# One value visit and one score fewer in two job words, and the gate's tanh behind the branch

## The chip, the cores and the metric

The kernel runs on one core of a Trainium2 chip. The metric is the device time of one execution in microseconds, as the median of several runs. Five engines work from queues of their own: TensorE (PE), VectorE (DVE), ScalarE (ACT), GpSimd (POOL) and SyncE (SP, which only issues DMAs here). Each works its queue in order, and they wait for one another by semaphores.

## The reference

```python
def _A_ref(x, wq, wk, wv, wo):          # 2048 tokens, D = 512, 32 heads of 16, one key/value head
    scores = jnp.einsum("bhqd,bkd->bhqk", q, k) * (Dh ** -0.5)
    p = _softmax(scores, axis=-1)
    o = jnp.einsum("bhqk,bkd->bhqd", p, v)
    ...
def _B_ref(x, w_gate, w_up, w_down):    # F = 1376
    return (_gelu(x @ w_gate) * (x @ w_up)) @ w_down

g = _sigmoid((x * gate_w).sum(-1, keepdims=True))
return g * a + (1 - g) * b              # a = attention, b = feed-forward
```

The kernel writes the sigmoid as a tanh: with t = tanh(z/2), g is 0.5t + 0.5 (tile `gt`) and 1 - g is -0.5t + 0.5 (tile `gc`).

## The kernel before, in words

**Prologue.** Weights and x are split into a high and a low part, and three matmuls per product keep the precision. The keys, the values and the queries are computed; the queries go through DRAM. Then a bound for the scores decides whether a softmax shift has to be computed: `values_load` of `flag` and `tc.If` (lines 514 and 515) make every engine load the flag and branch past a long body, which is not taken here. Between the last query matmul and the branch stand the first feed-forward chunk's gate and up products, its GELU's first step, the gate tanh (line 505) with its two DVE steps (lines 506 and 507), and the split of the second chunk's weights: three parts, each a cast on DVE and a subtraction on POOL.

**Main part.** Attention and feed-forward are interleaved by hand in one long stream of PE work. Attention is cut into 32 units of 16 key blocks, a *step* each: one unit is four heads of 512 queries. A step is two *scores* (`S`; each a pair of matmuls into a double bank `s`, then an exp on ACT from `s` to a tile `p` of 1024 columns, line 575) and one *value visit* (`V`; `pv`, line 645: four matmuls, recorded as eight, from the two `p` tiles into the accumulator `acc`). There are 1024 scores and 512 value visits. There is one accumulator bank: where a unit ends, `norm` copies it out on DVE (lines 586 and 596) before the next unit's first value visit may write it.

**Words.** The feed-forward and the output projection are cut into 81 *jobs*. Each has a pair of accumulators `z` and `y` and a stream of matmul pairs, `F`. A job is played by a word of the table `WORDS`: G for a gate/up job, D and E for the two halves of a down projection over three chunks, d and e for the same over two chunks, W for the output projection, L for the first gate/up job. In a word, `S3` means three scores, `V2` two value visits, `F6` six matmul pairs; `H` opens the pair and `R` closes it. `z` occupies the third of three double banks between `H` and `R`, so that scores then have two banks, taken in turn; at `R` that bank goes to the end of the turn. With no job left, `T` ("V2 S3") is played until all visits are done.

**The lead.** What the scores have issued ahead of the value visits is called the lead here, in steps: scores issued / 2 - visits made. `visit(k)` makes at most `ready` visits, those whose two scores have been issued, and carries the rest over to the next `V`. The lead is thus set when the program is written, not while it runs. At a lead of zero after a visit, that visit has read the exp of the score issued just before it.

**Order of jobs.** For each of the four groups of 512 tokens: G jobs with D E behind every third, then d e behind the last two chunks. Two W jobs for a group stand behind the next group's first D E.

Of the kernel before, what the change touches and what calls it, by code (L numbers as in the profile page):

```python
# [13 lines left out]
AF = mybir.ActivationFunctionType  # L14
ALU = mybir.AluOpType
# [5 lines left out]
S = 2048  # L21
D = 512
H = 32
DH = 16
F = 1376
# [14 lines left out]
EVERY = 3  # L40
PB = 12
WORDS = {
# [8 lines left out]
}  # L51

# [2 lines left out]
def mix_kernel(ctx, tc, xT, wq, wkv, wo, wf, out):  # L55
    nc = tc.nc
# [21 lines left out]
    zt = cp.tile([P, NKC], F32, name="zt")  # L78
    gt = cp.tile([P, NKC], F32, name="gt")
    gc = cp.tile([P, NKC], F32, name="gc")  # L80
# [37 lines left out]
    def split(eng_h, eng_l, hi, lo, src):  # L118
        if eng_h is nc.scalar:
            eng_h.copy(hi, src)  # L120
        else:
            eng_h.tensor_copy(hi, src)  # L122
        eng_l.tensor_sub(lo, src, hi)  # L123
# [87 lines left out]
    W = {}  # L211
# [4 lines left out]
    def defer(k, fn):  # L216
        later.setdefault(now[0] + k, []).append(fn)
# [6 lines left out]
    def split_w(n):  # L224
        if n not in stage:
            return []
        st = stage.pop(n)
        gh = cp.tile([P, 2, NC, P], F32R, tag="gh", name=f"gh{n}", bufs=2)
        gl = cp.tile([P, 2, NC, P], F32R, tag="gl", name=f"gl{n}", bufs=2)
        dh = cp.tile([P, D], F32R, tag="dh", name=f"dh{n}", bufs=4)  # L230
        dl = cp.tile([P, D], F32R, tag="dl", name=f"dl{n}", bufs=4)
        W[n] = gh, gl, dh, dl
        view = lambda t: st[:, t].rearrange("p (c f) -> p c f", c=NC)
        parts = [(gh[:, t], gl[:, t], view(t)) for t in range(2)] + [(dh, dl, st[:, 2])]
        return [lambda part=part: split(nc.vector, nc.gpsimd, *part) for part in parts]
# [96 lines left out]
    def flush(q):  # L332
        while q:
            q.pop(0)()
# [39 lines left out]
    def gelu(n, g, u):  # L374
        flush(chain)
        gs = cp.tile([P, TG], F32, tag="gs", name=f"gs{n}", bufs=1)
        sq = cp.tile([P, TG], F32, tag="sq", name=f"sq{n}", bufs=1)
        nc.vector.tensor_copy(gs, g)  # L378

        def inner():  # L380
            nc.vector.scalar_tensor_tensor(sq, gs, GC, gs, op0=ALU.mult, op1=ALU.mult)  # L381
            nc.vector.scalar_tensor_tensor(sq, sq, 1.0, gs, op0=ALU.add, op1=ALU.mult)

        def tanh():
            nc.scalar.activation(sq, sq, AF.Tanh, bias=0.0, scale=GS)  # L385

        def outer():
            nc.vector.scalar_tensor_tensor(sq, sq, 1.0, gs, op0=ALU.add, op1=ALU.mult)
            nc.vector.scalar_tensor_tensor(gs, u(), 0.5, sq, op0=ALU.mult, op1=ALU.mult)

        def halves():
            hh = cp.tile([P, TG], F32R, tag="hh", name=f"hh{n}", bufs=3)
            hl = cp.tile([P, TG], F32R, tag="hl", name=f"hl{n}", bufs=3)
            nc.vector.tensor_copy(hh, gs)
            nc.vector.tensor_sub(hl, gs, hh)
            hold.append((n, hh, hl))

        chain.extend((inner, tanh, outer, halves))

    def advance(m):  # L400
        def go():
            while len(chain) > m:
                chain.pop(0)()

        return go
# [83 lines left out]
    nsteps = 8 * NTG * NKC  # L489
# [12 lines left out]
    up0 = ps_a.tile([P, TG], F32, tag="pa", name="u0")  # L502
    chain_mm(up0, weights_terms(0, 1))
    gelu(0, ps, lambda: up0)
    nc.scalar.activation(gt, zt, AF.Tanh, bias=0.0, scale=0.5)
    nc.vector.tensor_scalar(gc, gt, -0.5, 0.5, op0=ALU.mult, op1=ALU.add)
    nc.vector.tensor_scalar(gt, gt, 0.5, 0.5, op0=ALU.mult, op1=ALU.add)
    for part in split_w(1):
        part()
    pro.close()  # L510
    mp = ctx.enter_context(tc.tile_pool(name="mp", bufs=1))
# [127 lines left out]
    def pv(s):  # L639
        u, kc = divmod(s, NKC)  # L640
        if kc == 0:
            accp[u] = ps_a.tile([P, TG], F32, tag="pa", name=f"acc{u}")
        vt = (v1, v2)[u % 2]
        for j in range(4):
            nc.tensor.matmul(accp[u][32 * j : 32 * j + 32], vt[:, kc], pb[s, j // 2][:, (j % 2) * TG : (j % 2 + 1) * TG],  # L645
                             start=(kc == 0), stop=(kc == NKC - 1), skip_group_check=True)
        del pb[s, 0], pb[s, 1]

    at_s, at_v, carry = [0], [0], [0]
# [5 lines left out]
    def visit(k):  # L655
        if at_v[0] == nsteps:
            return
        flush(chain if at_v[0] == 0 else [])
        want = k + carry[0]
        left = NKC - at_v[0] % NKC  # L660
        ready = at_s[0] // 2 - at_v[0]
        take = max(min(want, left, ready, 4), 0)
        if left - take == 1 and take < 3 and ready > take:
            take += 1
        carry[0] = want - take
        for _ in range(take):
            pv(at_v[0])
            at_v[0] += 1
        if take and at_v[0] % NKC == 0:
            if at_v[0] == nsteps:  # L670
                ends.append(None)
            else:
                norm(at_v[0] // NKC - 1)

    def play(word, job=None):
        if job:
            X, Y = job[1]()
        for t in word.split():
            k = int(t[1:] or 1)
            if t[0] == "S":  # L680
                for _ in range(k):
                    score()
            elif t[0] == "V":
                visit(k)
            elif t[0] == "H":
                advance(1)()
                held.add(2)
                z = ps_s.tile([P, 2 * TG], F32, tag="s2", name="z")[:, 0:TG]
                y = ps_f.tile([P, TG], F32, tag="pf", name="y")
                pairs = pair_mm(z, y, X, Y)  # L690
            elif t[0] == "F":
                for _ in range(k):
                    next(pairs)
            else:
                assert next(pairs, None) is None
                held.discard(2)
                turn.remove(2)
                turn.append(2)
                job[2](z, y)

    ends = []
    chain.pop(0)()
    for k, m in ((2, 2), (4, 0)):
        defer(k, advance(m))
    for job in jobs():
# [60 lines left out]
```

## Time and profile before

| | us |
|---|---|
| median of 3 runs (lowest, highest) | 1322.84 (1322.68, 1323.7) |
| profiled execution | 1322.12 |
| its span, first to last instruction | 1320.3 |
| PE busy | 1286.6 |
| ACT busy | 1034.9 |
| DVE busy | 573.7 |
| POOL busy | 221.4 |
| mean granted clock of TensorE | 0.995 |

Matmuls are pipelined and their ends are modelled: a PE that counts as busy may be waiting inside a value visit for half of its input. Where a job's length matters, it is read from the start of the job's first pair to the start of the next job's, as a stretch of the trace. A window's answer gives its length, then for each engine the busy time and the number of records, the granted clock, and the DMA's share and rate.

### The profile page before, as it was taken

The numbers are of one execution on the slowest core, as the hardware profiler recorded it, in microseconds if no ns is written. First come the engines' busy times: TensorE is split into PE (matmuls) and PEld (weight loads), VectorE is DVE, ScalarE is ACT, GpSimd is POOL, SyncE is SP. The second block draws the span as 40 slices with busy tenths as digits, with TensorE's granted clock in tenths as the row PEclk, the third lists the DMA queues.
The fourth block names the chain that finished last, engine by engine and source line by source line (L and its number), as shares of the span: only waits on it lengthen the run. The fifth ranks groups of instructions, "written<-read, shape, count | busy, mean of one in ns | idle before, by whom it ended". The sixth has DMA issues, their size and how long they took to land.

```text
span 1320.3 us, 23905 instructions
## 1 busy us (share of the span) xinstructions
PE 1286.6 (97%) x9884; PEld 663.8 (50%) x9884; DVE 573.7 (43%) x860; ACT 1034.9 (78%) x1118; POOL 221.4 (17%) x261
## 2 busy tenths in 40 slices
PE   9989999999999999999899999999999999999998
PEld 6854555454444454455355445554544445445544
DVE  6762543534541162624535145252644324344333
ACT  5368888887777888888687788888877788888883
POOL 3141202122210120202211012120222002112100
PEclk9989999999999999999999999999999999999999
DMA  8541112011100201111110021011121002110000
GB/s 310 184 131 38 62 37 62 27 53 53 62 14 30 76 27 38 62 38 53 53 51 12 30 77 62 14 63 36 54 65 37 14 30 87 50 34 32 14 1 32
DMA packets 26371, 72.67 MB, mean 55 GB/s; under 512 B 4016, under 2 KB 4048, under 8 KB 26256
## 3 DMA queue, kind: packets, MB, share of 16 engines
q1 hardware_dynamic: 25244, 69.17, 15.9%
q8 instruction: 80, 1.31, 0.4%
q10 hardware_dynamic: 756, 1.11, 0.3%
q0 software_dynamic: 256, 0.79, 0.1%
q14 instruction: 35, 0.29, 0.1%
HBM read 57.67 MB, written 13.37 MB: 54 GB/s over the span
## 4 chain that ended last, share of the span: by engine, by line
PE 88%; ACT 2%; POOL 1%; DVE 1%; issue 1%; DMA 0%; SPq 0%; ACTq 0%; DVEq 0%
PE acc L645 36%; PE z L353 24%; PE s L572 21%; PE y L353 6%; ACT p L575 2%; POOL gl L123 1%; PE wos L338 1%; DMA Q<-scr 0%; DVE n L596 0%; DVE acc L460 0%; PE wof L338 0%; DVE n L586 0%; POOL mark L361 0%; ACT sq L385 0%; DVE sq L381 0%
## 5 line engine op out<-in xcount | busy, mean ns | idle before, releaser
L575 ACT ACTIVATE p<-s 128x1024 f32<-128x1024 f32 x1024 | 981.5, 1024 | 226.7 <-PE s L572 219.9
L645 PE MATMUL acc<-p,v 128*32 128x512 f32 x4096 | 516.5, 601 | 8.4 <-DVE n L586 4.1
L572 PE MATMUL s<-Q,kp 51*128 51x512 f32 x2048 | 385.2, 420 | 13.1 <-ACT p L575 7.3
L572 PEld LDWEIGHTS s<-Q,kp 51*128 51x128 f32 x2048 | 183.2, 185 | 239.7 <-ACT p L575 139.2
L645 PEld LDWEIGHTS acc<-p,v 128*32 128x32 f32 x4096 | 108.2, 109 | 270.4 <-issue 221.7
L123 POOL TENSOR_TENSOR gl<-st,gh 128x512 fp32r<-128x512 f32 x88 | 124.8, 1439 | 378.2 <-DVE gh L122 136.2
L378 DVE COPY gs<-z 128x512 f32<-128x512 f32 x43 | 29.7, 692 | 282.3 <-PE y L353 273.8
L353 PE MATMUL z<-xh,gh 64*128 64x512 f32 x344 | 144.1, 419 | 1.2 <-POOL mark L361 0.9
L353 PE MATMUL y<-xh,gh 64*128 64x512 f32 x344 | 144.0, 419 | 0.0
L353 PE MATMUL y<-xl,gh 64*128 64x512 f32 x344 | 135.3, 393 | 0.0
L353 PE MATMUL z<-xl,gh 64*128 64x512 f32 x344 | 135.3, 393 | 0.0
L353 PE MATMUL y<-xh,gl 64*128 64x512 f32 x344 | 133.9, 389 | 0.0
L353 PE MATMUL z<-xh,gl 64*128 64x512 f32 x344 | 133.9, 389 | 0.0
L361 POOL MEMSET mark<- 1x1 f32 x81 | 8.1, 100 | 664.6 <-PE y L353 659.9
L353 PEld LDWEIGHTS z<-xh,gh 64*128 64x128 f32 x344 | 63.9, 186 | 59.7 <-ACT p L575 25.9
L450 DVE SCALAR_TENSOR_TENSOR acc<-z,gc,acc 128x512 f32<-128x512 f32 x24 | 18.0, 751 | 172.5 <-PE z L353 113.8
L353 PE MATMUL z<-dh,hh 64*128 64x512 f32 x176 | 70.4, 400 | 5.9 <-ACT p L575 5.9
L353 PEld LDWEIGHTS z<-xh,gl 64*128 64x128 f32 x344 | 64.2, 186 | 12.8
L353 PE MATMUL y<-dh,hh 64*128 64x512 f32 x176 | 70.6, 401 | 0.0
L353 PEld LDWEIGHTS z<-xl,gh 64*128 64x128 f32 x344 | 64.4, 187 | 10.8
L353 PE MATMUL y<-dh,hl 64*128 64x512 f32 x176 | 68.9, 391 | 0.0
L353 PE MATMUL z<-dh,hl 64*128 64x512 f32 x176 | 68.8, 391 | 0.0
(147 smaller groups left out, 1581.3 us busy)
## 6 DMA issues: line engine op xcount, KB each, us to landing
st<-wf SPq DMA_DIRECT2D x44, 768.0 KB
scr<-q SPq DMA_DIRECT2D x16, 512.0 KB
Q<-scr SPq DMA_DIRECT2D x60, 128.0 KB
out<-acc SPq DMA_DIRECT2D x16, 256.0 KB
Q<-scr SPq DMA_DIRECT2D x60, 64.0 KB
xr<-xT SPq DMA_DIRECT2D x6, 512.0 KB
xst<-xT SPq DMA_DIRECT2D x12, 256.0 KB
xr<-xT SPq DMA_DIRECT2D x4, 256.0 KB
```

The costliest lines, as they stand in the source:

```text
L123: eng_l.tensor_sub(lo, src, hi)
L338: nc.tensor.matmul(ps, a, b, start=(first and q == 0), stop=(last and q == len(terms) - 1), skip_group_check=True)
L353: mm = nc.tensor.matmul(ps, a[rs], b[rs], start=(half == 0 and q == 0), stop=(half == 1 and q == len(X) - 1), skip_group_check=True)
L361: relay = nc.gpsimd.memset(mark, 0.0).ins
L378: nc.vector.tensor_copy(gs, g)
L450: nc.vector.scalar_tensor_tensor(o, ps, w, o, op0=ALU.mult, op1=ALU.add)
L572: nc.tensor.matmul(ps[:, j * TG : (j + 1) * TG], kp[rs, kc * P : (kc + 1) * P], Q[u][rs, pr], start=True, stop=True)
L575: nc.scalar.activation(p, ps, AF.Exp, bias=0.0, scale=SCALE)
L645: nc.tensor.matmul(accp[u][32 * j : 32 * j + 32], vt[:, kc], pb[s, j // 2][:, (j % 2) * TG : (j % 2 + 1) * TG], start=(kc == 0), stop=(kc ...
```

## The change

Two edits in the table change what is issued: the word W has one score less at its end ("S R S2" becomes "R S2"), and the word e one visit less at its start ("V S V S V S H" becomes "S V S V S H"). In L the first of the two scores ahead of `H` moves behind it. ("F6 S2 F6" and "F6 S S F6" are the same stream.) There are six W jobs and four e jobs; what they no longer issue comes at the end, in `T`.

Around the branch, the gate tanh and its two DVE steps are put off by five scores, and the third part of the second chunk's split (`dh` and `dl`) is issued behind the branch. `ends` was a list that nothing reads.

```diff
 WORDS = {
-    "L": "S2 H F3 S F3 S F6 S2 F6 S F6 R S",
+    "L": "H S F3 S F3 S F6 S S F6 S F6 R S2",
     "G": "V2 S2 V H V F S2 F6 S F3 S F2 S F3 S F3 S F6 R S2 V2 S3 V",
-    "W": "V2 S2 H V2 S F S F6 S F2 S V S F3 S V S F S V S F2 S F3 S V S F6 S R S2",
+    "W": "V2 S2 H V2 S F S F6 S F2 S V S F3 S V S F S V S F2 S F3 S V S F6 R S2",
     "D": "V H V S2 V2 S2 F6 S F3 S V S F S F5 S F3 S R",
-    "E": "V S3 H V3 S F3 S F6 S2 F6 S F3 R S V2 S3",
+    "E": "V S3 H V3 S F3 S F6 S S F6 S F3 R S V2 S3",
     "d": "V S V H S F3 S F3 S V S F2 S F4 R",
-    "e": "V S V S V S H F3 S F3 S V2 S F5 S F R S",
+    "e": "S V S V S H F3 S F3 S V2 S F5 S F R S",
 }
...
     gelu(0, ps, lambda: up0)
-    nc.scalar.activation(gt, zt, AF.Tanh, bias=0.0, scale=0.5)
-    nc.vector.tensor_scalar(gc, gt, -0.5, 0.5, op0=ALU.mult, op1=ALU.add)
-    nc.vector.tensor_scalar(gt, gt, 0.5, 0.5, op0=ALU.mult, op1=ALU.add)
-    for part in split_w(1):
+    rest = split_w(1)
+    for part in rest[:2]:
         part()
...
-            if at_v[0] == nsteps:
-                ends.append(None)
-            else:
+            if at_v[0] < nsteps:
                 norm(at_v[0] // NKC - 1)
...
-    ends = []
+    def gates():
+        nc.scalar.activation(gt, zt, AF.Tanh, bias=0.0, scale=0.5)
+        nc.vector.tensor_scalar(gc, gt, -0.5, 0.5, op0=ALU.mult, op1=ALU.add)
+        nc.vector.tensor_scalar(gt, gt, 0.5, 0.5, op0=ALU.mult, op1=ALU.add)
+
+    rest[2]()
     chain.pop(0)()
+    defer(5, gates)
```

**DVE's queue at the branch**, before (the copy of the first gate product, the two gate steps, the split's three casts, the load of the flag, the branch):

```order
L313 TENSOR_SCALAR woh<-woh,sh 1x2048
L378 COPY gs_658<-g_622 128x512
L506 TENSOR_SCALAR gc<-gt 128x16
L507 TENSOR_SCALAR gt<-gt 128x16
L122 CAST gh_664<-st_191 128x512 x2
L122 CAST dh_666<-st_191 128x512
L514 TENSOR_LOAD flag
L515 COMPARE_AND_BRANCH
```

and now (the long body between the two branches is left out of the second piece, which begins at its end):

```order
L313 TENSOR_SCALAR woh<-woh,sh 1x2048
L378 COPY gs_658<-g_622 128x512
L122 CAST gh_661<-st_191 128x512 x2
L512 TENSOR_LOAD flag
L513 COMPARE_AND_BRANCH
```

```order
L513 UNCONDITIONAL_BRANCH x2
L122 CAST dh_663<-st_191 128x512
L381 SCALAR_TENSOR_TENSOR sq_659<-gs_658 128x512
L382 SCALAR_TENSOR_TENSOR sq_659<-sq_659,gs_658 128x512
L388 SCALAR_TENSOR_TENSOR sq_659<-sq_659,gs_658 128x512
```

The gate's steps and the third cast have left the queue ahead of the branch, and the cast now stands ahead of the GELU's steps behind it. On ACT the GELU's tanh (L385) now comes ahead of the first exp instead of behind it, and the gate tanh behind the fourth.

**PE's queue where the first e job opens** (`z` and `y` are the job's accumulators; `x4` on the `acc` row is one value visit), before:

```order
L353 MATMUL y<-dh_7191,hl_7530 128x512
L645 MATMUL acc_7533<-p,v_74 32x512 x4
L572 MATMUL s<-Q_7084,kp 128x512 x2
L645 MATMUL acc_7533<-p,v_74 32x512 x4
L572 MATMUL s<-Q_7084,kp 128x512 x2
L645 MATMUL acc_7533<-p,v_74 32x512 x4
L572 MATMUL s<-Q_7084,kp 128x512 x2
L353 MATMUL z<-dh_6756,hh_7353 128x512
```

and now:

```order
L353 MATMUL y<-dh_6756,hl_7354 128x512
L353 MATMUL z<-dh_7191,hh_7529 128x512
L353 MATMUL y<-dh_7191,hh_7529 128x512
L353 MATMUL z<-dl_7192,hh_7529 128x512
L353 MATMUL y<-dl_7192,hh_7529 128x512
L353 MATMUL z<-dh_7191,hl_7530 128x512
L353 MATMUL y<-dh_7191,hl_7530 128x512
L570 MATMUL s<-Q_7084,kp 128x512 x2
L643 MATMUL acc_7533<-p,v_74 32x512 x4
L570 MATMUL s<-Q_7084,kp 128x512 x2
L643 MATMUL acc_7533<-p,v_74 32x512 x4
L570 MATMUL s<-Q_7084,kp 128x512 x2
```

One visit is gone. From here to the W jobs, each visit stands one step further behind its scores than before.

**PE's queue at the end of the first W job**, before:

```order
L353 MATMUL y<-woh,ol_8462 128x512
L572 MATMUL s<-Q_8309,kp 128x512 x6
L645 MATMUL acc_8697<-p,v_75 32x512 x8
L572 MATMUL s<-Q_8309,kp 128x512 x4
L645 MATMUL acc_8697<-p,v_75 32x512 x8
```

and now:

```order
L353 MATMUL y<-woh,ol_8458 128x512
L570 MATMUL s<-Q_8304,kp 128x512 x4
L643 MATMUL acc_8691<-p,v_75 32x512 x4
L570 MATMUL s<-Q_8304,kp 128x512 x4
L643 MATMUL acc_8691<-p,v_75 32x512 x8
L570 MATMUL s<-Q_8304,kp 128x512 x2
```

Three scores in a row have become two.

## The prediction

> **What bounds the kernel now.** The page first:
>
> ```profile
> span 1320.3 us, 23905 instructions
> L575 ACT ACTIVATE p<-s 128x1024 f32<-128x1024 f32 x1024 | 981.5, 1024 | 226.7 <-PE s L572 219.9
> ```
>
> The exps occupy ACT for 981.5 us of 1320.3 and ACT's idle time is spent waiting for scores from PE, so over the whole PE's stream sets the time. But a PE that counts as busy may be waiting, so I went on to the timeline of PE. Here are two scores followed by two value visits at the end of a G job, at 143 us and at 327 us:
>
> ```profile
> 143.22 0.73 PE L572 MATMUL s<-Q,kp 51*128 51x512 f32 x4
> 143.88 1.92 PE L645 MATMUL acc<-p,v 128*32 128x512 f32 x16
> ...
> 326.70 0.73 PE L572 MATMUL s<-Q,kp 51*128 51x512 f32 x4
> 327.36 2.98 PE L645 MATMUL acc<-p,v 128*32 128x512 f32 x16
> ```
>
> The same sixteen records take 1.92 us in one place and 2.98 in the other. I counted scores and visits along PE's order list: behind the first pair the lead is 1, behind the second 0. At lead 0 the last visit reads the exp of the score issued just ahead; two exps in a row (2 x 1.02) outlast the visit before it. So a lead of zero costs PE 1.06 us wherever it happens, and it need not happen: ACT isn't full.
>
> Where does the lead fall to zero? The words say it: e issues 8 scores and 5 visits, one visit more than its scores feed, so each of the first three e jobs takes a step from the lead; W issues 17 scores for 8 visits, and the two W jobs give the step back. Between them lie three G jobs, a D and an E. The table of stretches, first three G jobs at full lead, then the three behind each e:
>
> ```profile
> 129.60:178.60 49.00, 48.99 (x402) 25.70 (x404) 25.83 (x38) 41.79 (x46) 9.85 (x10) 1.00 0.13 42
> 330.30:384.60 54.30, 52.32 (x402) 25.74 (x402) 28.74 (x44) 42.00 (x45) 11.28 (x12) 1.00 0.14 45
> 659.20:712.60 53.40, 53.27 (x406) 26.46 (x404) 26.42 (x39) 41.96 (x46) 9.82 (x10) 0.98 0.12 39
> 978.10:1030.70 52.60, 52.39 (x402) 25.73 (x402) 26.77 (x39) 41.76 (x45) 11.73 (x12) 1.00 0.12 39
> ```
>
> The second number is the length. Work is equal (42 scores, 21 visits and 72 pairs each), ACT is busy for 42 us in all four, and the length grows from 49.0 to 54.3, 53.4 and 52.6.
>
> **The change part by part.** With one visit less in e, the order list has the lead behind the visits of the first G job after e at 4.5, 3.5, 4, 3, 2, 2, 1 where it was 3.5, 2.5, 3, 2, 1, 1, 0: the list of the jobs at 129.6. The step is no longer given back because W loses two scores per group. No visit before the program's last one is left at lead 0. What goes away is waiting; PE's work stays the same, moved.
>
> *G jobs behind e*: 54.30 + 53.40 + 52.60 - 3 x 49.00 = 13.3 us. ACT's cover for this is 49.0 - 41.8 = 7 us of slack per three jobs; without it the gain would be nothing.
>
> *E jobs*: at full lead, and the first and the last of the three that follow an e (the middle one is as long):
>
> ```profile
> 116.90:129.60 12.70, 12.70 (x106) 6.10 (x102) 4.90 (x8) 10.51 (x11) 2.91 (x3) 1.00 0.09 39
> 396.50:410.50 14.00, 14.00 (x110) 6.67 (x108) 1.41 (x2) 10.51 (x11) 0.09 (x1) 1.00 0.00 1
> 1043.40:1057.40 14.00, 14.00 (x108) 6.70 (x106) 1.41 (x2) 10.51 (x11) 0.09 (x1) 1.00 0.00 1
> ```
>
> 3 x 1.3 = 3.9 us. The third G jobs in two triples of the second group end at a lead one visit lower as well, which the new list mends:
>
> ```profile
> 161.90:178.60 16.70, 16.70 (x142) 8.87 (x140) 12.02 (x18) 13.97 (x16) 2.90 (x3) 1.00 0.00 1
> 484.20:501.60 17.40, 17.04 (x142) 8.85 (x140) 9.22 (x15) 14.38 (x16) 1.55 (x3) 1.00 0.23 70
> ```
>
> 0.7 us each, 1.4 together. Small ones of this kind in the last group are left to the range.
>
> *W jobs.* The end of one on PE, and the page of waits for PE:
>
> ```profile
> 444.51 0.63 PE L572 MATMUL s<-Q,kp 51*128 51x512 f32 x4
> 446.08 0.51 PE L572 MATMUL s<-Q,kp 51*128 51x512 f32 x2 [0.95 <-ACT p L575]
> ...
> PE s L572 <- ACT p L575: 7.3, 13, 1.0
> ```
>
> Two scores take 2 x 0.23 us, so the third was due at 444.97 and came at 446.08, 1.11 late: `z`'s bank has gone to the end of the turn, the third score gets the bank of the first, and waits for its exp. With one score fewer the last one meets a bank whose exp was issued before the six pairs ahead. All six W jobs end so; 6 x 0.95 is 5.7 of the 7.3 us in the last row. 6 x 1.11 = 6.7 us. The first W job has a visit at lead 0 besides:
>
> ```profile
> 410.50:431.50 21.00, 19.65 (x148) 9.06 (x146) 2.98 (x5) 16.34 (x17) 0.09 (x1) 1.00 0.13 46
> 431.50:450.90 19.40, 18.45 (x148) 8.36 (x144) 3.50 (x5) 16.29 (x17) 2.91 (x3) 1.00 0.21 70
> ```
>
> With the second as its measure, 1.6; I take 1.4, since the leads differ. W: 8.1 us.
>
> *e jobs*, the first and the second, and the second's worst place:
>
> ```profile
> 318.60:330.30 11.70, 11.66 (x88) 4.66 (x88) 5.58 (x7) 6.86 (x7) 5.13 (x5) 1.00 0.30 91
> 643.80:659.20 15.40, 12.29 (x86) 4.75 (x86) 9.31 (x12) 6.86 (x7) 6.96 (x6) 0.85 0.36 96
> 653.39 1.64 DVE L621 TENSOR_TENSOR ol<-nt,oh 128x512 fp32r<-128x512 f32 x1
> 654.94 0.68 DVE L586 COPY n<-acc 128x512 f32<-128x512 f32 x1
> 655.68 3.64 PE L645 MATMUL acc<-p,v 128*32 128x512 f32 x16 [3.11 <-DVE n L586]
> ```
>
> Each of three e jobs has one visit at lead 0: 3 x 1.06 = 3.2. In the second a unit ends, and its copy on DVE stands behind two other steps; the next unit's visit waits 3.11 us, and the clock drops (0.85). In the new list that unit's end has a whole G stream between it and the next visit: 15.40 - 11.70 = 3.7. Together 6.9 us.
>
> *Unit ends elsewhere.* One bank for `acc` means that where two visits meet across a unit's end, PE waits for the copy:
>
> ```profile
> 464.53 1.06 PE L645 MATMUL acc<-p,v 128*32 128x512 f32 x7 [0.81 <-DVE n L596]
> ```
>
> Such a meeting costs 0.81 us to 1.0. Before there are four of them; the new list has three (in the last group), and several ends at which two scores lie between. I take them as even. Bounds: 0.8 gained, and per end up to the 3.11 above lost.
>
> *The end.* Four visits and six scores now come behind the last job, as two more rounds of T without pairs between them. ACT there:
>
> ```profile
> 1297.41 2.86 ACT L575 ACTIVATE p<-s 128x1024 f32<-128x1024 f32 x3 [0.82 <-PE s L572]
> 1300.99 2.86 ACT L575 ACTIVATE p<-s 128x1024 f32<-128x1024 f32 x3 [0.72 <-PE s L572]
> ```
>
> A round takes 3.58 us at low lead and can't take less than ACT's 2.86; PE's work in it is 0.73 + 0.23 + 1.92 less overlap, about 2.75, and that is only moved. The loss is 2 x 0.1 to 2 x 0.8; with a lead of 3 to start from, near the lower end: 0.6.
>
> *The start.* The timeline around the branch, DVE's part of line 515, and the clock:
>
> ```profile
> 70.08 0.21 ACT L505 ACTIVATE gt<-zt 128x16 f32<-128x16 f32 x1 [5.70 <-DMA Q<-scr]
> 70.33 0.17 DVE L506 TENSOR_SCALAR gc<-gt 128x16 f32<-128x16 f32 x1 [2.24 <-ACT gt L505]
> 71.29 1.49 DVE L122 CAST dh<-st 128x512 fp32r<-128x512 f32 x1
> 74.40 1.42 PE L572 MATMUL s<-Q,kp 51*128 51x512 f32 x4 [5.73 <-DVEq L515]
> 75.48 1.02 ACT L575 ACTIVATE p<-s 128x1024 f32<-128x1024 f32 x1 [5.18 <-DMA st<-wf]
> 76.67 0.86 PE L572 MATMUL s<-Q,kp 51*128 51x512 f32 x2
> ...
> L515 DVEq COMPARE_BRANCH  x1: 72/72/72, 71.2 to 71.2; - x1
> L515 DVEq EVENT_SEMAPHORE  x1: 21/21/21, 74.3 to 74.3; - x1
> ...
> 68.60:74.40 5.80, 0.07 (x2) 0.03 (x1) 2.42 (x6) 0.21 (x1) 3.28 (x3) 0.69 0.35 113
> 74.40:78.40 4.00, 4.00 (x21) 3.71 (x23) 3.17 (x4) 2.92 (x4) 0.72 (x1) 0.59 0.66 207
> ```
>
> PE and ACT wait for DVE, which reaches its branch at 71.2 and needs 3.1 us to get across. It was late because its queue waited 2.24 us for the gate tanh. Without that it reaches the branch about 3 us earlier and is across near 71.4, PE starts near 71.6, 2.8 earlier. Not all of it stays. DVE now does the cast (0.4 to 1.49) and two GELU steps before ACT's tanh, and the first exp stands behind that tanh on ACT: about 74.5 to 75.5, against 75.48 to 76.5. The third score needs that exp's bank: about 75.5 instead of 76.67, with three pairs more done: 1.2 + 3 x 0.23 = 1.9 us. If the half clock of the last row lasts as long as now, more work falls under it, and about 1.4 is left; if PE does not cool, 2.4. I take 1.9. The gate's own steps (0.21 and twice 0.17) land in idle time; `gc` is first read by the first D job. No DMA is issued by what moves; POOL's subtraction goes behind the branch with its cast, and SP's next weight fetch waits for it as before.
>
> On the clock: the first of the two stretches has 0.69 on average, which is half speed for 3.6 of its 5.8 us, so it fell about 2.2 us into the gap. [...]
>
> **Sum**: 13.3 + 3.9 + 1.4 + 8.1 + 6.9 + 1.9 - 0.6 = 34.9 us. The profiled execution took 1322.12 us around its span of 1320.3, the median is 1322.84; the same gain from the median gives 1287.9, said as 1288.
>
> **Rivals.**
> *ACT takes over.* If PE only waits because ACT can't keep up, a lead moves each wait to the next bank. Then only the W ends, the collision in the second e and the start count: 6.7 + 3.7 + 1.9 = 12.3, 1310.5. For it: ACT is 83% busy in an E job. Against: the E job at full lead has the same 10.51 us of ACT within 12.70. 5%.
> *Late copies.* Unit ends have moved, and some may meet DVE steps that POOL slows, as in the second e. Four at 3.1: 12.4 lost, 1300.7. Against: before, one of 31 was that late. 14%. [...]
> *The start gives nothing*, since cast, GELU and tanh now stand ahead of the first exp: 1290.2. 10%.
> *Slower*: the accumulator's single bank becomes the bound. Twelve of the 31 unit ends late by 3.1 are 37 us, and from there on the gain is gone: 1325. 3%.
> *The change doesn't do what it says*: the carry in `visit` could make up the dropped visit. The order lists, which end with four more visits, speak against it: 1320, 1%.
>
> My forecast has the remaining 67%. Its own range is 1283 to 1294, from the start's ends, the last group's unlisted mends (up to 3) and one or two late copies. For 8 in 10 with the milder rivals, 1281 to 1299. A measurement of this kernel tells about 0.2%, 2.6 us, from no change; by the cases faster has 96%, same 1%, slower 3%.
>
> **What would show it.** Right: three G jobs behind each e at 49 us, E at 12.7, no visit pair of 2.98 us except at the very end, no 0.95 us wait at the ends of W, the first score near 71.6. Wrong: waits of `acc` for `n` on DVE above 1 us in several places; stretches still at 53 us with ACT busier than 42; a first exp later than 75.5.

## The result, and the profile after

The changed kernel takes **1287.05 us** as the median of four runs (1286.57 to 1287.82), beside 1322.76 us for the kernel before in the runs taken with it. The ratio is 0.9732, with a 95% interval of 0.9715 to 0.9749. The forecast was 1288.0. The profiled execution has a span of 1286.0 us, 34.3 less than before.

The sum is met, but not by its own terms: the start, forecast to gain 1.9 us, lost 1.6 in this trace, and the jobs gained 2.9 more than was listed. The page of the changed kernel, its span and the three costliest groups:

```profile
span 1286.0 us, 23903 instructions
...
L573 ACT ACTIVATE p<-s 128x1024 f32<-128x1024 f32 x1024 | 981.9, 1024 | 187.1 <-PE s L570 185.3
L643 PE MATMUL acc<-p,v 128*32 128x512 f32 x4096 | 496.9, 599 | 3.6 <-DVE n L584 2.3
L570 PE MATMUL s<-Q,kp 51*128 51x512 f32 x2048 | 384.0, 419 | 4.7 <-SPq L513 3.0
```

The exps cost what they did, 981.9 us. What shrank is ACT's idle time ahead of them, from 226.7 to 187.1 us: PE hands over its scores sooner. Neither engine does less work. The stretches of the changed kernel (length, then busy time and records of PE, weight loads, DVE, ACT and POOL, the granted clock, the DMA's share and rate): the three G jobs behind the first, second and third e job, an E job, the first two W jobs, and two stretches behind the branch:

```profile
329.70:379.00 49.30, 49.15 (x402) 25.72 (x404) 26.37 (x39) 41.99 (x45) 12.67 (x13) 1.00 0.16 50
638.50:687.90 49.40, 49.13 (x402) 25.67 (x404) 26.96 (x41) 41.90 (x45) 12.45 (x13) 1.00 0.13 42
947.00:997.00 50.00, 49.19 (x402) 25.53 (x404) 27.73 (x40) 41.92 (x46) 12.92 (x13) 1.00 0.12 41
...
390.80:403.80 13.00, 13.00 (x110) 6.57 (x108) 1.41 (x2) 10.54 (x11) 0.09 (x1) 1.00 0.01 1
403.80:422.10 18.30, 18.30 (x148) 8.50 (x146) 2.98 (x5) 15.39 (x16) 0.09 (x1) 1.00 0.13 43
422.10:440.00 17.90, 17.90 (x146) 8.17 (x142) 3.50 (x5) 15.54 (x16) 2.91 (x3) 1.00 0.21 67
...
72.29:74.73 2.44, 1.46 (x8) 1.03 (x9) 1.99 (x2) 0.38 (x1) 1.48 (x1) 0.85 0.56 186
74.73:80.90 6.17, 6.17 (x30) 6.09 (x31) 2.50 (x4) 3.74 (x5) 0.09 (x1) 0.50 0.51 184
```

The triples have come from 54.3, 53.4 and 52.6 to 49.3, 49.4 and 50.0 with the same 41.9 to 42.0 us of ACT in them. The timeline of PE in the changed kernel, in order: the wait ahead of the first e job, the end of a W job, the end of the second e job, the one new meeting inside a G triple, and the last visits of the program:

```profile
317.37 0.50 PE L570 MATMUL s<-Q,kp 51*128 51x512 f32 x2
319.05 0.49 PE L353 MATMUL z<-dh,hh 64*128 64x512 f32 x1 [1.18 <-ACT p L573]
...
435.03 0.63 PE L570 MATMUL s<-Q,kp 51*128 51x512 f32 x4
435.59 1.92 PE L643 MATMUL acc<-p,v 128*32 128x512 f32 x16
...
652.53 0.73 PE L570 MATMUL s<-Q,kp 51*128 51x512 f32 x4
653.19 1.92 PE L643 MATMUL acc<-p,v 128*32 128x512 f32 x16
...
976.75 1.06 PE L643 MATMUL acc<-p,v 128*32 128x512 f32 x8 [0.81 <-DVE n L594]
...
1266.12 0.96 PE L570 MATMUL s<-Q,kp 51*128 51x512 f32 x6
1267.01 3.67 PE L643 MATMUL acc<-p,v 128*32 128x512 f32 x16
```

The W job ends with two scores and goes straight into its visits. The visit pair of 2.98 us has become one of 1.92. Only the program's last pair (3.67 us) still runs dry. The page of waits for PE in the changed kernel, rows of over 0.9 us in total that lie behind the prologue (total, times, longest):

```profile
PE z L353 <- ACT p L573: 5.6, 6, 1.2
PE s L570 <- SPq L513: 3.0, 1, 3.0
PE acc L643 <- DVE n L584: 2.3, 4, 1.0
PE acc L643 <- DVE n L594: 1.3, 4, 0.8
...
PE s L570 <- issue: 1.0, 1, 1.0
```

Before, scores waited 7.3 us for exps and a visit 3.11 us for a late copy. The late copy is gone, and of the 7.3 us one wait of 0.7 is left, inside the last W job. The first row stayed: between a d and its e the first pair waits for an exp in four places (1.45 us against the usual pace in each).

**The start.** The timeline around the branch in the changed kernel:

```profile
68.92 0.39 PE L338 MATMUL u<-xh,gl 128*128 128x512 f32 x1
...
71.43 0.59 DVE L122 CAST dh<-st 128x512 fp32r<-128x512 f32 x1 [2.03 <-DVEq L513]
...
72.29 0.75 PE L570 MATMUL s<-Q,kp 51*128 51x512 f32 x2 [2.98 <-SPq L513]
...
73.36 0.39 PE L353 MATMUL y<-xh,gl 64*128 64x512 f32 x1
74.35 0.63 ACT L385 ACTIVATE sq<-sq 128x512 f32<-128x512 f32 x1 [9.31 <-DVE sq L382]
74.73 0.80 PE L570 MATMUL s<-Q,kp 51*128 51x512 f32 x2 [0.98 <-issue]
74.89 1.92 ACT L573 ACTIVATE p<-s 128x1024 f32<-128x1024 f32 x2
```

and the sequencers at the branch (the last numbers are the starts of the first and the last record):

```profile
L513 SPq EVENT_SEMAPHORE  x8: 17/17/17, 71.6 to 72.2; - x8
L513 DVEq COMPARE_BRANCH  x1: 72/72/72, 67.9 to 67.9; - x1
...
L513 DVEq EVENT_SEMAPHORE  x1: 21/21/21, 71.3 to 71.3; - x1
```

DVE is at its branch at 67.9, 3.3 us earlier than before, and across at 71.3. PE does not start then: its first score waits for SP, whose eight signals behind the branch go out between 71.6 and 72.2, and starts at 72.29. It issues one score and six matmuls, stands still from 73.75 to 74.73 for nothing that the profile shows, and goes on at half clock until 80.9. From the last matmul ahead of the branch to the first D job it takes 37.8 us (68.92 to 106.72), where it was 36.8 (68.28 to 105.08). This interval is called the start in what follows. It scatters: kernels whose start is written as before show 36.8, 37.0, 37.4 and 37.6. The last matmul itself came 0.64 us later than before (68.92 against 68.28), ahead of everything that was changed. Counted from it, the first score came after 3.37 us, 6.12 before.

### The profile page after: what moved, and what is told of

It is laid out like the page before. It is cut to its first block, busy times and chain, and to the rows that moved or that the text cites. A ratio compares the mean times of both kernels' runs of the same rounds, so it can differ in the third digit from the quotient of the medians.

```text
span 1286.0 us, 23903 instructions
## 1 busy us (share of the span) xinstructions
PE 1265.1 (98%) x9884; PEld 664.9 (52%) x9884; DVE 575.2 (45%) x860; ACT 1035.5 (81%) x1118; POOL 222.0 (17%) x261
## 3 DMA queue, kind: packets, MB, share of 16 engines
q10 hardware_dynamic: 756, 1.11, 0.3%
## 4 chain that ended last, share of the span: by engine, by line
PE 90%; DVE 2%; ACT 1%; POOL 1%; issue 1%; ACTq 0%; DVEq 0%
PE acc L643 36%; PE z L353 24%; PE s L570 21%; PE y L353 7%; ACT p L573 1%; POOL gl L123 1%; PE wos L338 1%; DVE n L584 0%; DVE n L594 0%; DVE acc L460 0%; DVE ol L619 0%; PE wof L338 0%; DVE gh L122 0%; DVE oh L615 0%; DVE sq L382 0%
## 5 line engine op out<-in xcount | busy, mean ns | idle before, releaser
L573 ACT ACTIVATE p<-s 128x1024 f32<-128x1024 f32 x1024 | 981.9, 1024 | 187.1 <-PE s L570 185.3
L643 PE MATMUL acc<-p,v 128*32 128x512 f32 x4096 | 496.9, 599 | 3.6 <-DVE n L584 2.3
```

What stands on the lines that cost most here:

```text
L573: nc.scalar.activation(p, ps, AF.Exp, bias=0.0, scale=SCALE)
```

## Experiments

**Which of the two edits does it?** One kernel has the two shorter words alone, with the old start:

```diff
-    "W": "... S V S F6 S R S2",
+    "W": "... S V S F6 R S2",
-    "e": "V S V S V S H F3 ...",
+    "e": "S V S V S H F3 ...",
```

> The kernel before with the new words W and e alone; the branch, the gate's tanh and L stay as before. Theory (the lead and the ends of W make the gain; the moves around the branch lose the 1.6 us by which the first D job starts later in the changed kernel's trace, 106.7 against 105.1): about 1285.4, with the first D job at 105.1 and the rest as in the changed kernel. Rival (the moves around the branch gain 1.9 us, as predicted, and that trace met a bad phase of the clock): about 1289.

Measured: 1287.51 us, ratio 0.9736 (0.9720 to 0.9752). That is the whole gain. The 1285.4 of the theory was missed: the first D job came at 106.03, not at 105.1, so the old start was slow in this trace too. From the first D job on, its stretches are those of the changed kernel. The other kernel has the new code around the branch, and the words L, W and e of before:

```diff
-    "L": "H S F3 S ... F6 R S2",
+    "L": "S2 H F3 S ... F6 R S",
-    "W": "... F6 R S2",
+    "W": "... F6 S R S2",
-    "e": "S V S V S H F3 ...",
+    "e": "V S V S V S H F3 ...",
```

> The changed kernel with the old words L, W and e: only the gate's tanh with its two DVE steps and the third part of the split stand behind the branch. Theory (a start that comes earlier on PE meets a cold clock, a late tanh and a pause of instructions): 0 to 2 us slower than before, 1322.8 to 1324.5, no change at the old leads otherwise. Rival (the start gains, and only the reordered L loses it again): about 1321.

Measured: 1320.99 us, ratio 0.9986 (0.9976 to 0.9995), some 1.7 us less, as the rival had it; the theory, slower than before, is out. Its first score is at 71.63, where the prediction had it, but its start is 37.5 us, no shorter than with the old code. What its profiled execution gained lies elsewhere: the visit behind the late copy in the second e job. The stretch behind that wait of 3.11 us, in this kernel:

```profile
649.00:656.18 7.18, 4.07 (x35) 1.66 (x31) 5.79 (x8) 4.70 (x5) 2.80 (x2) 1.00 0.76 198
656.18:660.00 3.82, 3.82 (x33) 2.07 (x35) 3.80 (x5) 1.12 (x2) 2.83 (x2) 1.00 0.00 0
```

and in the kernel before:

```profile
648.40:655.68 7.28, 4.17 (x37) 1.72 (x33) 5.79 (x8) 4.79 (x5) 2.80 (x2) 0.92 0.73 195
655.68:660.00 4.32, 4.32 (x20) 1.25 (x22) 3.77 (x5) 0.00 (x0) 2.79 (x2) 0.50 0.00 0
```

The same wait let the clock fall in one trace and not in the other. How the 1.7 us of the medians divide between such luck and the start, these runs don't tell. The start's worth lies between nothing and 1.7 us.

**Is it a bank at the ends of W?** The same three scores are issued, but the first of them stands three pairs earlier, so that `z`'s release no longer meets three in a row:

```diff
-    "W": "... S V S F6 S R S2",
+    "W": "... S V S F3 S F3 R S2",
```

> The kernel before with one score of W moved three pairs ahead: 'F6 S R S2' becomes 'F3 S F3 R S2'. No score and no visit less, every lead as before. Theory (the third score in a row waits for a bank whose exp has just begun, 1.11 us in each of six jobs): 6 to 6.7 us faster, about 1316.4. Rival (the wait only moves to the next bank): 1322.8.

Measured: 1317.79 us, ratio 0.9962 (0.9947 to 0.9976), 4.9 us less than before. The end of the second W job in this kernel:

```profile
444.96 0.39 PE L572 MATMUL s<-Q,kp 51*128 51x512 f32 x2
445.61 0.50 PE L572 MATMUL s<-Q,kp 51*128 51x512 f32 x2 [0.26 <-ACT p L575]
```

The last score comes 0.65 us behind the one ahead of it, where 0.23 is the pace: 0.42 late instead of 1.11, and alike in five of the six ends (0.56 in the first). The mechanism is the bank. Moving a score by three pairs leaves 0.4 us of each wait, and dropping it leaves nothing. In the profiles the six W jobs gain 4.1 us; the rest of the difference is not theirs. The expected 6 to 6.7 was missed by the 0.4 that stays.

**Is the lead what matters?** Only W loses its score. Then each group takes a step of lead that nothing gives back:

```diff
-    "W": "... S V S F6 S R S2",
+    "W": "... S V S F6 R S2",
```

> The kernel before with the new word W alone; e keeps its fifth visit. The W ends gain 6.7 us, but the step that e takes is no longer given back, and the order list has 114 visits at lead 0 where before has 21. Theory (a visit at lead 0 costs up to 1.06 us, less where pairs stand between its score and it): 93 more visits at 0.4 to 1.06 us, less 6.7: slower, 1353 to 1414. Rival (the surplus visit costs only where it stands, once per e): about 1316.

Measured: 1447.51 us, ratio 1.0943 (1.0925 to 1.0961). The kernel has the same work in another order, 114 visits at lead 0 where there were 21, and loses 125 us. The page of waits for PE, and what the weight loads of the visits waited for, in this kernel:

```profile
PE acc L645 <- ACT p L575: 40.9, 49, 1.0
...
  ACT p L575: 245.4, 322
```

In the kernel before the first row had 1.0 us and the last 32.4. The direction was as expected, the size was not: 125 us instead of at most 91. Gaps between PE's instructions against the usual pace: 91 us stand inside visits at lead 0, about 0.9 each, as expected (before has 21 such visits, with 16 us), but 43 us stand ahead of 44 visits that take the lead from 1 to 0, about 1.0 each. The first half of such a visit reads the last exp but one and has to wait for it too; I had priced only the wait for the last one.

Shortening e alone was not tried, so that its part of the gain is read from the traces and not measured by itself. W would then give more than e takes, the scores would run ahead of the visits by a step in every group, and they would soon want a thirteenth `p` tile of twelve.

**Why is the start no shorter?** The changed kernel with the old L, two scores ahead of the first pair:

```diff
-    "L": "H S F3 S F3 S F6 S S F6 S F6 R S2",
+    "L": "S2 H F3 S F3 S F6 S2 F6 S F6 R S",
```

> The changed kernel with the old word L: the moves around the branch and the new words W and e stay. Four traces with the old start have the first D job 36.8 to 37.6 us behind the last matmul ahead of the branch, two with the new start 37.5 and 37.8. Theory (the start is worth nothing either way, within what the clock's phase does): 1286 to 1288, the first D job 36.8 to 37.8 us behind that matmul. Rival (L's new order loses about 1 us of what the earlier branch gains): 1285.5 or less, the D job below 36.8.

Measured: 1285.54 us, ratio 0.9725 (0.9709 to 0.9742). The start is 36.1 us, the first score at 71.50, and the pause behind it 0.17 us. Against the changed kernel that is 1.5 us by the medians and 0.9 by the ratios (the runs of before were at 1322.02 here), with intervals that overlap, and 1.7 us of the start in the profiles. These are the rival's numbers, but they don't show that the new order in L costs: the kernel with the new branch code and all old words has the same instructions from the branch to the first D job, and its start was 37.5. That kernel pauses for 0.66 us, and the half clock lasted 10.24 us in its trace and 6.83 in this one:

```profile
74.57 0.79 PE L353 MATMUL z<-xh,gl 64*128 64x512 f32 x1 [0.66 <-issue]
```

What the new L does cost is seen in the first G job behind it, from its first pair to the first D job, in the kernel before and in the changed one:

```profile
88.19:105.08 16.89, 16.71 (x136) 8.86 (x138) 11.02 (x16) 14.04 (x15) 8.30 (x7) 1.00 0.16 57
...
88.92:106.72 17.80, 17.19 (x137) 9.65 (x139) 11.88 (x17) 14.89 (x16) 8.30 (x7) 1.00 0.25 89
```

All eight traces with the old L have 16.9 us there, all five with the new one 17.5 to 17.8. Whether L itself gives this back, the scatter of the start hides. To see what the pause is, 32 matmuls are added to the long body that the branch skips. They are never run, and only push the code behind the branch to another place:

```diff
-                for i in range(4):
+                for i in 3 * list(range(4)):
                     nc.tensor.transpose(...)
```

> The changed kernel with 32 matmuls more in the body behind the branch, which is not run: what is executed is the same, but PE's code behind the join lies elsewhere in its 16 KB blocks. In the changed kernel PE stands still from 73.4 to 74.7 us with nothing that it waits for, while a 16 KB block on the instruction queue lands at 73.45. Theory (PE waits for its next block of instructions): the pause moves or goes, the third score comes at 76.0 or earlier instead of 76.39, 0.3 to 1 us faster. Rival (the pause is a hidden wait for a bank or a semaphore): it stays at the same matmul.

Measured: 1285.30 us, ratio 0.9722 (0.9706 to 0.9738). The scores behind the branch in this kernel:

```profile
71.45 0.99 PE L570 MATMUL s<-Q,kp 51*128 51x512 f32 x2 [2.79 <-SPq L513]
...
73.23 0.92 PE L570 MATMUL s<-Q,kp 51*128 51x512 f32 x2
...
75.56 0.50 PE L570 MATMUL s<-Q,kp 51*128 51x512 f32 x2 [0.30 <-ACT p L573]
```

The second score comes at 73.23 instead of 74.73 with no wait in front, the third at 75.56 (the prediction said about 75.5), and the start is 35.6 us. So the pause of 0.98 us was PE waiting for its own next instructions. The traces' records agree. In the changed kernel a block of 16 KB on the queue that carries instructions lands at 73.45, and PE goes on 1.28 us later. The two unpadded kernels with the new branch code and the old L go on 1.41 and 1.34 us behind such a landing (73.16 to 74.57, 72.60 to 73.94). In this kernel the block lands at 72.51, while PE still works, and none of the three padded kernels has the pause. Not all of the 2.2 us that the start is shorter need be the pause: the half clock lasts 3.41 us in this trace (71.53 to 74.94) and 6.83 in that of the changed kernel (74.01 to 80.84). The times don't settle the gain either, as the intervals of the ratios overlap. What the traces show of crossing the branch is 3.4 us for DVE in the changed kernel, a branch of PE that ends 1.35 to 1.36 us behind the landing of a 16 KB block in all twelve kernels that have it, and up to 0.98 us of pause where a second such block lands late (73.45).

For the clock's part, the kernel with the two shorter words alone, with 24 idle matmuls ahead of the branch. They are run and read by nothing:

```diff
+    wm = ps_f.tile([P, TG], F32, tag="pf", name="wm")
+    for _ in range(24):
+        nc.tensor.matmul(wm, warm[:, 0:P], warm, start=True, stop=True)
     pro.close()
```

> The new words W and e with the old start, and 24 idle matmuls on zeros put ahead of the branch on PE, which fill its gap of 6 us. Theory (the half clock behind the branch comes from that gap and costs 1.5 to 2.5 us): granted clock 1.00 from 70 to 84 us, 1285 to 1286. Rival (the exps set the pace there, a cold PE is hidden): 1287.5 as without.

Measured: 1286.44 us, ratio 0.9731 (0.9714 to 0.9747), 1.1 us below the two words alone by the medians, 0.7 by the ratios. The stretches around the branch in this kernel:

```profile
68.57:74.77 6.20, 5.36 (x25) 2.30 (x25) 3.28 (x6) 0.22 (x1) 3.99 (x3) 1.00 0.44 140
74.77:80.00 5.23, 4.76 (x34) 3.36 (x36) 3.95 (x7) 4.29 (x5) 0.02 (x1) 1.00 0.48 164
```

The clock stays whole, and the start is 36.8 us where the two words alone had 37.6. But the kernel before has 36.8 as well, with the same start and a half clock. So the half clock is worth between nothing and 1 us here, and the runs can't tell. Why it is not more is not shown; ACT, whose exps PE waits for behind it, is the likely reason.

Without the branch there would be nothing to cross. One kernel leaves the load of the flag and the body out, so it lacks the fallback that computes the softmax shift when the bound asks for it. It has the e word of the next experiment:

```diff
-    v = nc.values_load(flag[0:1, 0:1], min_val=0, max_val=1)
-    with tc.If(v > 0):
-        ...
```

> The changed kernel with the new order at the start of e and without the branch: flag is not loaded and the shift for large scores is left out of the program. Theory (the branch itself holds PE from the last matmul to the first score, 3.4 us in the changed kernel, and half of its cold clock): first score 2 us or less behind the last matmul ahead of it, no pause, about 1277. Rival (the DMA of the shift row and the queries sets the start): first score 2.5 us or more behind, 1279.

Measured once: 1283.01 us, slower than both expectations. The first score is at 73.88, later than with the branch, for the rival's reason:

```profile
68.66 4.45 ACTq L315 DMA_DIRECT2D kp<-woh  x2
L315 ACTq DMA_DIRECT2D kp<-woh x2: 505/560/616, 68.7 to 72.6; - x2
...
73.88 1.40 PE L531 MATMUL s<-Q,kp 51*128 51x512 f32 x2 [5.10 <-DMA kp<-woh]
```

It waits for the two small rows that ACT writes into `kp` (line 315). The first was issued at 68.66, as ever (69.03 in the changed kernel), but the second only at 72.6 (69.7 in the changed kernel). And now the fetch of the next weights, which used to stand behind the branch on SP (72.29 in the changed kernel), has gone out at 65.72. The stretch that follows has the DMA engines busy for 0.84 of the time, at 246 GB/s, and the next one hardly at all:

```profile
68.00:72.00 4.00, 0.78 (x4) 0.32 (x2) 3.45 (x6) 0.00 (x0) 3.38 (x2) 0.93 0.84 246
72.00:73.88 1.88, 0.00 (x0) 0.03 (x1) 0.06 (x1) 0.63 (x1) 1.82 (x2) 0.50 0.09 16
```

In the changed kernel they are at 0.26 and 65 GB/s between 68.92 and 72.29. So it is the second issue on ACT's queue that is late. That the early fetch is the reason is read from this and not shown by a run of its own. The branch was holding that fetch back: without its 3 us, another thing is late.

**The wait that stayed.** Four times 1.45 us are lost where an e job opens: its pair `z` waits for the exp of a score issued two ahead. `H` is put one score earlier, which takes the bank whose exp is older:

```diff
-    "e": "S V S V S H F3 ...",
+    "e": "S V S V H S F3 ...",
```

> As the run before it, and in the word e the last score ahead of H moves behind it ('S V S V H S F3'), so that the z pair does not open in a bank whose exp has just begun. The changed kernel's trace has PE wait 1.45 us there in each of the four e jobs. Theory (that wait goes whole): 5 to 5.8 us faster than the run before it, about 1280. Rival (the score behind H then waits instead): no gain.

Measured, on top of the idle matmuls: 1280.77 us, ratio 0.9688 (0.9672 to 0.9704), 5.7 us below them alone (4 x 1.45 is 5.8). The place in this kernel that answers to 317.37 above:

```profile
315.69 0.50 PE L575 MATMUL s<-Q,kp 51*128 51x512 f32 x2
316.03 0.39 PE L353 MATMUL z<-dh,hh 64*128 64x512 f32 x1
```

The same word on top of the padded kernel:

> The changed kernel with the 32 matmuls in the body that is not run and the new order at the start of e ('S V S V H S F3'). If both gains stand side by side: 1285.3 - 5.7 = 1279.6. If the e gain needs the warm start of the run in which it was tried: 1283 or more.

Measured: 1280.64 us, ratio 0.9682 (0.9665 to 0.9698), near the 1279.6 of two gains side by side and far from 1283. With 13 idle matmuls ahead of the branch besides:

> As the run before it, with 13 idle matmuls (2.9 us at full clock) ahead of the branch on PE. Theory (the half clock behind the branch still costs PE 1 to 2 us of the start): granted clock 1.00 from 70 to 80 us, about 1278.5. Rival (with the tanh ahead of the first exp, the exps set the pace there whatever PE's clock): 1279.6, no gain.

Measured: 1280.56 us, ratio 0.9685 (0.9669 to 0.9701): no gain, as the rival had it. The three can't be told apart. All beat the kernel before by 3.1 to 3.2% and the changed kernel by about 6 us. In the last the clock is whole (1.00) and the start 35.6 us (36.5 without the idle matmuls), but the medians are the same: its runs go from 1279.63 to 1281.83, and a gain of under a microsecond drowns in that.

## Why the prediction was right, and where it was wrong

By its own steps, from the starts of all jobs in both traces (work that only moved is left out; how much stands under unit ends and how much under unlisted mends was divided by hand):

| step | predicted | measured |
|---|---|---|
| G behind e | 13.3 | 11.8 |
| E | 3.9 | 3.1 |
| third G's of the second group | 1.4 | 1.4 |
| W | 8.1 | 8.3 |
| e | 6.9 | 6.8 |
| unit ends | 0 | 1.5 |
| end | -0.6 | -0.5 |
| unlisted mends | in the range, up to 3 | 3.5 |
| start | 1.9 | -1.6 |
| sum | 34.9 | 34.3 |

- **G behind e: right in kind, 1.5 too high.** The first two triples came to 49.3 and 49.4, nearly the 49.0 taken as measure. The third triple has one of the new meetings of two visits at a unit's end (976.75, 0.81 us of wait), which I had counted among the unit ends.
- **E: 0.8 too high.** I measured against the first E job, 12.70 us. The others now take 12.97, and what the remaining 0.3 is stays open.
- **W: right in sum and in mechanism.** The bank's wait is gone in all six, and moving the score instead of dropping it (1317.79) shows that it was the bank. Without the score that moved, the last W job gained only 0.4, as it has a new gap of 0.87 us at 1047.8; the first gained 2.5.
- **e: right.** The three visits at lead 0 and the collision of 3.7 us are gone. No copy of a unit is late anywhere in the new trace: the longest wait for one is 1.0 us.
- **Unit ends: not even, but 1.5 better.** Three meetings in the second group went (2.4 us) and three came, of which one stands in the G row and two cost 0.9 net of small mends in the same jobs.
- **Unlisted mends: at the edge of what the range had room for.** Most are jobs behind the third e that work from a higher lead, 0.2 to 0.7 us each.
- **The start: wrong, in sign for this trace.** The failing step is "across near 71.4, PE starts near 71.6 [...] about 75.5 instead of 76.67, with three pairs more done". DVE was across at 71.3, as said, and counted from the last matmul ahead of the branch the first score came as said too: 3.37 us behind it where the forecast has 3.32 (68.28 to 71.6). That matmul was 0.64 late, where nothing was changed. What the step lacked came behind the first score. PE waited 0.98 us for its next instructions, so that the second score came at 74.73. And the half clock, which before lay half on the gap (3.3 us of it on work: 4.0 us at 0.59), now lay wholly on work for 6.17 us; 2.9 us more at half speed are at most 1.4 us. At the first G job, 20.00 us behind the last matmul where it was 19.91, the 1.9 and 0.1 more were gone, which these two, 2.4 at most, can cover. The first G job itself then took 0.9 longer (17.80 against 16.89), a term that the step did not have; what in the new order of L makes it so is open. Together, 0.64 + 2.0 + 0.9 is the 3.5 between the forecast and the trace. The step's upper end of 2.4 was for a PE that does not cool; no run without idle matmuls shows that. In all five traces that have the new branch code and no idle matmuls the clock fell to half, behind waits of 2.79 to 3.49 us for the first score.
- **The rivals.** *ACT takes over* is out: ACT is busy for 42 us in triples of 49. *Late copies* and *slower* did not come. That DVE steps are slowed beside POOL, as the first of them has it, is in the traces: in the kernel before the cast of `dh` takes 0.41 us at 659.03, with POOL at rest, and 1.49 at 71.29, beside POOL's subtraction (71.12 to 73.89); the step of 1.64 us, which began beside such a subtraction, has a median of 0.68. *The start gives nothing* came true for the start alone, and the unlisted mends hid it in the sum.

That the result lies within 1 us of the forecast is thus partly luck: 3.5 us too much on the start, 2.9 too little on the jobs.

## What to carry to other kernels

Where two producers and a consumer are interleaved by hand, count what each word gives to and takes from the lead, over the whole order: a surplus visit in three jobs cost some 22 us (the G, E and e rows above), because it was given back only five jobs later and the consumer ran dry in each in between. Price a dry lead by two waits, not one: one ahead of the visit that brings it to zero (about 1.0 us here) and one inside it (about 0.9). A wait removed ahead of a branch is worth something only if all engines that matter cross it sooner and the code behind it is there in time; read first who is next to arrive (here DVE came 3.3 us earlier, and PE then waited for SP until 72.29 and 0.98 us for its own instructions). And one trace of a start that scatters by a microsecond doesn't price a change in it.

## What the runs showed of the hardware that was not expected

- Crossing a branch over a long body that is not run cost DVE 3.4 us in the changed kernel from its comparison to its first signal, and PE met a second pause of 0.98 us about 1.5 us behind its first score. 32 matmuls of code that never runs, put ahead, took this pause away in three kernels. What it is worth in time is not clear of the noise: 1.3 us by the ratios (0.9732 to 0.9722, with intervals of 0.0034), 1.75 by the medians.
- The granted clock fell to 0.50 within a gap of 5.8 us about 2.2 us after its beginning (at 70.85 in the kernel before), and at a wait of 3.11 us in one trace (0.50 in the stretch behind it, kernel before) and not in another with the same wait (1.00, new branch code with old words). In the changed kernel it fell at 74.01, behind a gap of 2.98 us and with PE at work again since 72.29. The length of the gap alone doesn't decide it here. Behind the branch the half clock lasted 3.41, 6.83 or 10.24 us (padded kernel, kernel before, new branch code with old words), in these three a multiple of 3.41, which may be part of why one start scatters.
- Taking out the branch made the start later. A transfer that had been held back by it (768 KB of weights) went out 3 us ahead of one of 8 KB that PE was waiting for, and PE could start only when that one had landed, at 73.88.
